# Dilated q and k of the first two batches in rows of eight, masks made by GpSimd, and batch 0's sums in banks of their own

## The chip, the cores and the metric

One core of one Trainium2 chip. The metric is the device time of one execution in microseconds (us). A kernel is timed in several rounds, each beside the kernel before on the same chip; a median is quoted with the lowest and highest run.

## The reference

Eight batches, eight heads, 576 tokens of 64 values. Heads 0 to 3 look back over 32 tokens ("plain"), heads 4 to 7 over every fourth of the last 128 ("dilated"). The output of the attention goes through a feed-forward block with a gate.

```python
mask_plain = (rel >= 0) & (rel < window)                 # rel = query - key, window = 32
mask_dil = (rel >= 0) & (rel < window * dilation) & (rel % dilation == 0)   # dilation = 4
scores = np.where(masks, scale * q @ k.T, -1e9)          # heads 0-3 plain, 4-7 dilated
attn = softmax(scores) @ v
x = attn.transpose(0, 2, 1, 3).reshape(B * S, H * D)     # 4608 x 512
g = x @ w_gate                                           # 512 x 1536
out = (gelu(g) * (x @ w_val)) @ w_out                    # 1536 x 512
```

## The kernel before

The tokens go through the feed-forward in nine chunks of 512. PE (TensorE) works on the attention of the next batch between the matmuls of a chunk. Batch 0's attention has nothing to hide behind, so it is a serial start: load q and k, cast to f16, transpose on PE, add the mask as a bias by a matmul, scores, exp on ScalarE, denominators and numerators on PE, normalisation on DVE (VectorE). The weights come in three pairs (gate and value) and three output blocks, issued by GpSimd's queue. Batch 1's q and k wait for the second pair (`gate`), so that they are not in flight beside it (it lands at 31.2 us, k's load follows at 31.64).

```python
def quads(src, b, h0, lo, hi):                 # four tokens in a partition: 1 KB runs, 128 partitions
    return src[b, h0 : h0 + HK, lo:hi, :].rearrange("h (p r) d -> p h (r d)", r=4)

for t, src, eng in ((0, q, nc.sync), (1, k, nc.scalar)):
    eng.dma_start(out=first_p[:, t], in_=sixes(src, 0))            # plain heads
nc.gpsimd.dma_start(ident, id_dram.ap())                           # constants come by DMA
nc.gpsimd.dma_start(mask_p, mp_dram.ap())
for t, src, eng in ((0, q, nc.sync), (1, k, nc.scalar)):
    eng.dma_start(out=fh(first_d[t]), in_=quads(src, 0, HK, 0, 4 * P))
    eng.dma_start(out=fh(first_r[t]), in_=quads(src, 0, HK, 4 * P, S))   # the last 64 tokens
nc.gpsimd.dma_start(ident32, id32_dram.ap())
nc.gpsimd.dma_start(mask_d, md_dram.ap())
# ... v, tiles
warm(16, 7)
# ... casts and transposes of the plain heads; bias_p by DVE, bias_d by GpSimd
load_v_dil_rest(0)
load_w(0)
v_cast(0, sv0)                                  # waits for v
copy("pool", tiles["v", 0][1], r4(first_vd))
w1 = load_w(1)
load_w(2)
# ...
emit_s(0, 4, pe_mask=True)                      # scores and exp of head pair 0
emit_s(1, 0, pe_mask=True)
# ... casts of dilated k
den(0, 4, wide=True)
# ... t_dil, t_rest: transposes of the dilated heads
den(1, 4, wide=True)
emit_s(2, 0, pe_mask=True)
num(0, 4)
# ...
gate["dma"] = w1
for t, src in ((0, q), (1, k)):
    gated(nc.sync.dma_start(out=st1[:, t], in_=sixes(src, 1)))
qd1, rd1 = load_qk_dil(1)                       # rows of four, cast in the DMA
load_wo(0)
# ... GpSimd casts q and k of batch 1 (needs st1)
wo1 = load_wo(1)
wo2 = load_wo(2)
```

The softmax here doesn't subtract the row's maximum and nothing guards it: scores larger than these inputs give would overflow.

Of the kernel before, what the change touches and what calls it, by code (L numbers as in the profile page):

```python
# [9 lines left out]
F16 = mybir.dt.float16  # L10
F32 = mybir.dt.float32
# [4 lines left out]
WIN = 32  # L16
DIL = 4
USCALE = 32.0


def _np_masks():
    p = np.arange(128)[:, None]

    def band(n, off=0):
        rel = np.arange(n)[None, :] + off - p
        return (rel >= 0) & (rel < WIN)

    main_p, last_p, tail_p = band(160), band(128), band(64, 64)
    main_d = band(128)

    rel = 48 + np.arange(16)[None, :] - p % 64
    rest_d = [(rel >= 0) & (rel < WIN) & (p // 64 == m) for m in range(2)]
    mp = np.concatenate([main_p, main_p, main_p, last_p, tail_p], axis=1).astype(np.float16)
    md = np.concatenate([main_d, rest_d[0], main_d, rest_d[1]], axis=1).astype(np.float16)
    return mp, md
# [3 lines left out]
def kernel(  # L39
# [19 lines left out]
    R6 = S // 6  # L59
    NCH = NT // CH  # L60
# [10 lines left out]

    mp_np, md_np = _np_masks()
    mp_dram = nc.inline_tensor(mp_np, name="mask_plain")
    md_dram = nc.inline_tensor(md_np, name="mask_dil")
    id_dram = nc.inline_tensor(np.eye(P, dtype=np.float16), name="attn_identity")
    id32_dram = nc.inline_tensor(np.eye(16, dtype=np.float32), name="identity_f32")
# [14 lines left out]
    ident32 = const.tile([16, 16], F32, tag="ident32")  # L91
# [20 lines left out]
    first_d = [x32[t][:, 0 : HK * 4 * D] for t in range(2)]  # L112
    first_r = [x32[2 + t][0:16, 0 : HK * 4 * D] for t in range(2)]
# [28 lines left out]
    def fh(t):  # L142
        return t.rearrange("p (h c) -> p h c", h=HK)

    def sixes(src, b):

        return src[b, 0:HK, :, :].rearrange("h (p r) d -> p h (r d)", r=6)

# [126 lines left out]
    def t_dil(b, hp, qd, q0, k0, engs):  # L275

        qtd_ = tiles["qT", b][1]
        for t, c0 in ((0, q0), (1, k0)):
            for hl in range(2):
                for m in range(2):  # L280
                    nc.tensor.transpose(
                        ps16f[:, c0 + (2 * hl + m) * P : c0 + (2 * hl + m + 1) * P],
                        qd[:, t, 2 * hp + hl, 2 * m : 2 * m + 2, :].rearrange("p r d -> p (r d)"),
                        ident,
                    )
        for t, c0 in ((0, q0), (1, k0)):
            copy(
                engs[t],
                qtd_[:, t, 2 * hp : 2 * hp + 2].rearrange("p h m i -> p (h m) i")[:, :, 0:P],
                ps16f[:, c0 : c0 + 512].rearrange("p (c i) -> p c i", i=P),  # L290
            )

    def t_rest(b, hp, rd, r0):

        qtd_ = tiles["qT", b][1]
        f32 = rd[0].dtype == F32
        pv = (psf if f32 else ps16f)[:, r0 : r0 + P]
        for t in range(2):
            for hl in range(2):
                for m in range(2):  # L300
                    c0 = (4 * t + 2 * hl + m) * 16
                    h0 = (2 * hp + hl) * 4 * D + 2 * m * D
                    nc.tensor.transpose(
                        pv[:, c0 : c0 + 16], rd[t][:, h0 : h0 + P], ident32 if f32 else ident[0:16, 0:16]
                    )
        nc.vector.tensor_copy(
            qtd_[:, :, 2 * hp : 2 * hp + 2].rearrange("p t h m i -> p t (h m) i")[:, :, :, P:NCL],
            pv.rearrange("p (t c i) -> p t c i", t=2, i=16),
        )
# [226 lines left out]
    nc.gpsimd.dma_start(ident, id_dram.ap())  # L536
    nc.gpsimd.dma_start(mask_p, mp_dram.ap())
    for t, src, eng in ((0, q, nc.sync), (1, k, nc.scalar)):
        eng.dma_start(out=fh(first_d[t]), in_=quads(src, 0, HK, 0, 4 * P))
        eng.dma_start(out=fh(first_r[t]), in_=quads(src, 0, HK, 4 * P, S))  # L540
    nc.gpsimd.dma_start(ident32, id32_dram.ap())
    nc.gpsimd.dma_start(mask_d, md_dram.ap())
# [5 lines left out]
    qd0 = ldp.tile([P, 2, HK, 4, D], F16, tag="qd", name="qd0")  # L548
    new_qt(0)



    def r4(t):
        return fh(t).rearrange("p h (r d) -> p h r d", r=4)

    warm(16, 7)
    for hp in range(2):
        for t in range(2):
            cast_six(("dve", "act")[t], q6, first_p, t, hp)
    nc.vector.tensor_scalar(bias_p, mask_p, 1.0, 60000.0, ALU.subtract, ALU.mult)  # L560
    for hp in range(2):
        t_plain(0, q6, hp, 2 * hp, ("act", "dve"))
    nc.gpsimd.tensor_scalar(bias_d, mask_d, 1.0, 60000.0, ALU.subtract, ALU.mult)
    for hp in range(2):
        copy("pool", qd0[:, 0, 2 * hp : 2 * hp + 2], r4(first_d[0])[:, 2 * hp : 2 * hp + 2])
    load_v_dil_rest(0)
    load_w(0)
    v_cast(0, sv0)
    copy("pool", tiles["v", 0][1], r4(first_vd))
    w1 = load_w(1)  # L570
    load_w(2)
# [8 lines left out]

    emit_s(0, 4, pe_mask=True)
    emit_s(1, 0, pe_mask=True)
    for hp, eng in ((0, "dve"), (1, "act")):
        copy(eng, qd0[:, 1, 2 * hp : 2 * hp + 2], r4(first_d[1])[:, 2 * hp : 2 * hp + 2])
    den(0, 4, wide=True)
    for hp in range(2):
        t_dil(0, hp, qd0, 4096 + 1024 * hp, 4608 + 1024 * hp, ("act", "dve"))
    for hp in range(2):
        t_rest(0, hp, first_r, P * hp)
    last_keys(0, 0, HK)  # L590
    den(1, 4, wide=True)
    emit_s(2, 0, pe_mask=True)
    num(0, 4)
    den(2, 4, wide=True)
    emit_s(3, 0, pe_mask=True)
    num(1, 4)
    den(3, 4, wide=True)
    num(2, 0)
    num(3, 2)

# [7 lines left out]
    qd1, rd1 = load_qk_dil(1)  # L608
# [28 lines left out]
    for c in range(NCH):  # L637
# [11 lines left out]
        for nb in range(NNB):  # L649
            if nb == 0 and c < 2:  # L650
                ffn1_two(c, (4, 6) if c == 0 else (6, 0))
            elif nb == 0 and late == "x":
                ffn1_two(c, pairs)
            elif nb > 1 or c > 2 and late != "x":
                ffn1(c, nb, pairs[(nb + swap) % 2])
            if pend is not None:
                norm_x(pend, SB)
                pend = None
            if nb in pv_at:
                pend = pv_at[nb]  # L660
                emit_pv(pend, SB, wide=True)
                norm_r(pend, SB, wide=True)
            if c == 0 and nb in (9, 10):
                t_plain(1, q61, nb - 9, 4 + 2 * (nb - 9), ("act", "dve"))
            if c == 0 and nb in (8, 11):
                rr = rd1.rearrange("p t h r d -> p t (h r d)")
                hp = nb // 11
                t_dil(1, hp, qd1, 4096 + 512 * hp, 5120 + 512 * hp, ("dve", "dve"))
                t_rest(1, hp, (rr[:, 0], rr[:, 1]), 6144 + P * hp)
            if nb == NNB - 1 and c > 0 and s_list:  # L670
                n = s_list.pop(0)
                masks.append(emit_s(n, SB, pe_mask=n in biased))
# [106 lines left out]
```

## Time and profile before

| | before |
|---|---|
| time, three runs | 363.44 us (363.22 to 364.12) |
| span in the profile | 362.5 us |
| PE busy | 95% of the span |
| first 16 feed-forward matmuls end | 29.85 us |
| first matmul with the output weights | 51.26 us |
| first feed-forward matmul of the second chunk | 69.03 us |

The last three rows are the milestones. They are read from PE's timeline (start, duration, operation; the wait before it in brackets). Between them lie the serial start, the first chunk's gate and value products, and its output products. In the prediction, the page's busy slices are fortieths of the span; the chain is the work that ended last, followed back to what released it. Of PE's waits up to 70 us, these are three of the four that the profile puts down to a load, as the last releaser, with total, number and longest (the fourth, for batch 1's dilated k, is 0.4 us):

```profile
PE ps L264 <- DMA ident<-attn_identity: 1.4, 1, 1.4
PE ps L281 <- DMA qd<-in_q_dram: 0.9, 1, 0.9
PE ps L512 <- DMA wo<-in_moe_w_out_dram: 0.7, 1, 0.7
```

The first stands in the start, the other two in the first chunk, where batch 1's dilated q and the last output weight are late.

### The profile page before, as it was taken

The numbers are of one execution on the slowest core, as the hardware profiler recorded it, in microseconds if no ns is written. First come the engines' busy times: TensorE is split into PE (matmuls) and PEld (weight loads), VectorE is DVE, ScalarE is ACT, GpSimd is POOL, SyncE is SP. The second block draws the span as 40 slices with busy tenths as digits, with TensorE's granted clock in tenths as the row PEclk, the third lists the DMA queues.
The fourth block names the chain that finished last, engine by engine and source line by source line (L and its number), as shares of the span: only waits on it lengthen the run. The fifth ranks groups of instructions, "written<-read, shape, count | busy, mean of one in ns | idle before, by whom it ended". The sixth has DMA issues, their size and how long they took to land.

```text
span 362.5 us, 6061 instructions
## 1 busy us (share of the span) xinstructions
PE 345.5 (95%) x2400; PEld 164.2 (45%) x2400; DVE 184.8 (51%) x278; ACT 146.0 (40%) x212; POOL 78.2 (22%) x110
## 2 busy tenths in 40 slices
PE   7879899999989999899999999999999999999995
PEld 2554354444544445444444444444444444444442
DVE  1585445744266325864477638783669413303320
ACT  1733255253543345434553356336542223312321
POOL 2580333540432332063003410240000000000000
PEclk9899999999999999999999999999999999999999
DMA  7999999999899898599438962893100030011002
GB/s 184 244 177 214 220 133 194 192 157 235 188 142 204 181 161 154 136 173 135 101 93 186 158 96 89 195 140 72 60 30 2 0 116 2 1 60 58 0 29 89
DMA packets 107292, 45.31 MB, mean 125 GB/s; under 512 B 83040, under 2 KB 102496, under 8 KB 107264
## 3 DMA queue, kind: packets, MB, share of 16 engines
q1 hardware_dynamic: 84272, 31.21, 39.8%
q0 software_dynamic: 21456, 12.01, 26.6%
q10 hardware_dynamic: 1536, 1.70, 2.0%
q8 instruction: 19, 0.31, 0.4%
q14 instruction: 9, 0.07, 0.1%
HBM read 40.13 MB, written 9.44 MB: 137 GB/s over the span
## 4 chain that ended last, share of the span: by engine, by line
PE 78%; DMA 13%; DVE 5%; POOL 2%; ACT 1%; issue 1%; ACTq 0%; SPq 0%; POOLq 0%; DVEq 0%
PE ps L481 41%; PE ps L512 25%; PE ps L433 5%; DMA xT<-in_k_dram 4%; DMA st<-in_k_dram 3%; PE ps L493 3%; DMA wv<-in_moe_w_val_dram 3%; DMA wo<-in_moe_w_out_dram 2%; DVE xT L469 2%; PE ps L360 1%; DMA sv<-in_v_dram 1%; PE ps L330 1%; DVE dt L451 1%; DVE rb L455 1%; PE ps L346 1%; POOL qp L251 1%
## 5 line engine op out<-in xcount | busy, mean ns | idle before, releaser
L506 DVE SCALAR_TENSOR_TENSOR u_all<-g,ps 128x512 f16<-128x512 f16 x108 | 73.5, 686 | 85.9 <-PE ps L481 76.9
L505 ACT ACTIVATE g<-ps 128x512 f16<-128x512 f32 x108 | 63.6, 597 | 126.0 <-PE ps L481 115.0
L512 PE MATMUL ps<-wo,u_all 128*128 128x512 f16 x432 | 101.1, 380 | 1.1 <-DMA wo<-in_moe_w_out_dram 0.7
L481 PE MATMUL ps<-xT,wg 128*128 128x512 f16 x392 | 100.7, 379 | 0.3
L481 PE MATMUL ps<-xT,wv 128*128 128x512 f16 x392 | 100.6, 379 | 0.0
L512 PEld LDWEIGHTS <-u_all 128*128 128x128 f16 x432 | 39.2, 98 | 45.4 <-issue 1.5
L481 PEld LDWEIGHTS <-wv 128*128 128x128 f16 x392 | 38.4, 98 | 46.4 <-issue 0.2
L481 PEld LDWEIGHTS <-wg 128*128 128x128 f16 x392 | 37.2, 98 | 45.0 <-issue 2.1
L523 ACT ACTIVATE osb<-ps 128x512 f32<-128x512 f32 x33 | 19.7, 597 | 49.0 <-PE ps L512 49.0
L451 DVE STREAM_TRANSPOSE dt<-ps 128x576 f32<-128x576 f32 x32 | 24.9, 779 | 26.2 <-PE ps L433 25.9
L190 POOL CAST qp<-st 128x2048 f16<-128x2048 f32 x6 | 11.4, 1894 | 99.0 <-DMA st<-in_k_dram 84.8
L455 DVE STREAM_TRANSPOSE rb<-rc 128x576 f32<-128x576 f32 x32 | 24.9, 778 | 1.1
L362 ACT ACTIVATE P<-ps 128x1152 f16<-128x1152 f32 x16 | 18.1, 1130 | 10.8 <-PE ps L360 10.8
L340 ACT ACTIVATE P<-ps 128x960 f16<-128x960 f32 x16 | 15.5, 970 | 10.7 <-PE ps L330 10.6
L469 DVE TENSOR_TENSOR xT<-ps,rb 128x576 f16<-128x576 f32 x16 | 17.9, 1126 | 0.3
L493 PE MATMUL ps<-xT,wg 128*128 128x512 f16 x40 | 15.2, 379 | 2.1 <-DVE xT L469 1.6
L525 DVE TENSOR_SCALAR osb<-ps 128x512 f32<-128x512 f32 x3 | 2.1, 691 | 28.8 <-PE ps L512 28.8
L433 PE MATMUL ps<-P,ones 128*64 128x96 f16 (+5 forms) x216 | 14.3, 245 | 1.6 <-ACT P L362 1.6
L493 PE MATMUL ps<-xT,wv 128*128 128x512 f16 x40 | 15.2, 379 | 0.0
L466 DVE TENSOR_TENSOR xT<-ps,rb 128x576 f16<-128x576 f32 x16 | 11.8, 745 | 0.3
L370 DVE TENSOR_TENSOR P<-P,mask_p 128x1344 f16<-128x1344 f16 x10 | 8.4, 852 | 6.8 <-ACT P L341 6.8
L370 DVE TENSOR_TENSOR P<-P,mask_d 128x1152 f16<-128x1152 f16 x8 | 6.1, 757 | 11.1 <-ACT P L362 11.1
(75 smaller groups left out, 244.2 us busy)
## 6 DMA issues: line engine op xcount, KB each, us to landing
out_dram<-osb SPq DMA_DIRECT2D x36, 256.0 KB, 2.1
sv<-in_v_dram SPq DMA_DIRECT2D x40, 128.0 KB, 3.2
st<-in_q_dram SPq DMA_DIRECT2D x24, 128.0 KB, 3.7
st<-in_k_dram SPq DMA_DIRECT2D x24, 128.0 KB, 3.1
qd<-in_q_dram POOLq DMA_DIRECT2D x7, 256.0 KB, 5.0
qd<-in_k_dram POOLq DMA_DIRECT2D x7, 256.0 KB, 6.9
vd<-in_v_dram POOLq DMA_DIRECT2D x7, 256.0 KB, 7.2
wg<-in_moe_w_gate_dram POOLq DMA_DIRECT2D x3, 512.0 KB, 7.4
```

The source lines that it names most:

```text
L340: nc.scalar.activation(pt[:, :, 0:PB], sb[:, 0, :, 0:PB], AF.Exp, bias=0.0, scale=scale)
L362: nc.scalar.activation(pt, ps[:, b0 : b0 + 4, 0:DW], AF.Exp, bias=0.0, scale=scale)
L433: nc.tensor.matmul(o, lhs, rhs, start=st, stop=True, skip_group_check=True)
L451: nc.vector.transpose(dst, den)
L455: nc.vector.transpose(rb.rearrange("p (b c) -> p b c", c=32), bass.AP(tensor=rc.tensor, offset=rc.offset, ap=[rc.ap[0], [1, 18], [0, 32]]),)
L469: nc.vector.tensor_tensor(dst.rearrange("p (i m s) -> p i m s", m=2, s=2), num, rb.rearrange("p (s m i) -> p i m s", s=2, m=2), ALU.mult,)
L481: nc.tensor.matmul(ps[:, b0 + gi, :], w[:, kc, ns], xT[kc][:, tok], start=(kc == 0), stop=(kc == NKC - 1))
L493: nc.tensor.matmul(ps[:, pairs[nb] + gi, :], w[:, kc, ns], xT[kc][:, tok], start=(kc == 0), stop=(kc == NKC - 1),)
L505: nc.scalar.activation(g, ps[:, b0, :], AF.Gelu)
L506: nc.vector.scalar_tensor_tensor(u_all[:, nb, :], g, USCALE, ps[:, b0 + 1, :], ALU.mult, ALU.mult)
L512: nc.tensor.matmul(ps[:, bank, :], u_all[:, fc, tb * P : (tb + 1) * P], wo_t[fc // 4][:, fc % 4, :], start=(fc == 0), stop=(fc == NNB - 1),)
L523: nc.scalar.activation(osb, ps[:, bank, :], AF.Copy, bias=0.0, scale=1.0 / USCALE)
```

## The change

Four parts with one intent, an earlier start: fewer and longer runs for dilated q and k; no constants over the DMA engines; more warm-up; sums that don't wait for one another's PSUM banks. The order of the weight loads moves with them.

```diff
-    nc.gpsimd.dma_start(ident, id_dram.ap())          # and mask_p, ident32, mask_d
+    nc.gpsimd.memset(ident, 1.0)
+    for sign in (1, -1):
+        nc.gpsimd.affine_select(out=ident, in_=ident, pattern=[[sign, P]], ...)
+    band(mask_p[...], 0, 0) ...                        # ten more selects
+    nc.gpsimd.tensor_scalar(bias_p, mask_p, 1.0, 60000.0, ALU.subtract, ALU.mult)   # was on DVE
 [...]
-        eng.dma_start(out=fh(first_d[t]), in_=quads(src, 0, HK, 0, 4 * P))
-        eng.dma_start(out=fh(first_r[t]), in_=quads(src, 0, HK, 4 * P, S))
+    for g in range(2):                                 # rows of eight: 72 partitions, 2 KB runs
+        for t, src, eng in ((0, q, nc.sync), (1, k, nc.scalar)):
+            eng.dma_start(out=first_d[t][g]..., in_=eights(src, 0, HK + 2 * g, HK + 2 * g + 2))
 [...]
-    warm(16, 7)
+    warm(20, 7)
 [...]
+    cast_d("pool", 0, 0)
+    cast_d("dve", 1, 0)
+    cast_d("act", 1, 1)          # ScalarE: second half of k, ahead of the exps
+    cast_d("dve", 0, 1)
     load_v_dil_rest(0)
     load_w(0)
-    v_cast(0, sv0)
-    copy("pool", tiles["v", 0][1], r4(first_vd))
     w1 = load_w(1)               # no longer behind v's casts
-    load_w(2)
 [...]
+    def num_split(n, b0):        # ScalarE copies out of PSUM, GpSimd multiplies
+        emit_pv(n, b0, ("num",))
+        nc.scalar.copy(first_n[n], psf[:, b0 * 512 : b0 * 512 + S])
+        nc.gpsimd.tensor_tensor(xT[n][:, 0:S], first_n[n], rb, ALU.mult)
     emit_s(0, 4, pe_mask=True)
     emit_s(1, 0, pe_mask=True)
+    t_dil(0, 0, qd0, 4, ("dve", "dve"))     # transposes of 72 columns, no remainders
+    t_dil(0, 1, qd0, 6, ("act", "act"))
 [...]                                       # v's casts
+    den(0, 0, wide=True)
+    den(1, -2, wide=True)
+    emit_s(2, 4, pe_mask=True)
+    emit_s(3, 0, pe_mask=True)
+    den(2, 4, wide=True)
+    num_split(0, 4)
+    num_split(1, 4)
     den(3, 4, wide=True)
     num(2, 0)
     num(3, 2)
+    load_w(2)                    # third pair behind GpSimd's products
 [...]
-    qd1, rd1 = load_qk_dil(1)
+    nc.gpsimd.dma_start(out=qd1[:, t]..., in_=eights(src, 1, HK, H))   # q and k of batch 1
```

## The prediction

> **What bounds the kernel now.** I read the page first: PE is busy for 95% of 362.5 us, so only time in which PE lacks work can be won. The chain's summary says the same and names the exceptions.
>
> ```profile
> PE   7879899999989999899999999999999999999995
> DMA  7999999999899898599438962893100030011002
> PE 78%; DMA 13%; DVE 5%; POOL 2%; ACT 1%; issue 1%; ACTq 0%; SPq 0%; POOLq 0%; DVEq 0%
> ```
>
> PE's thin slices lie at the start, and there the DMA engines are full; the DMA part of the chain (13%) lies there too. So I read the chain in order of time up to 54 us, where it turns into PE for good.
>
> ```profile
> 1.19 12.94 DMA xT<-in_k_dram
> ...
> 14.15 4.48 DMA sv<-in_v_dram
> ...
> 18.84 1.04 POOL vp L177
> ...
> 21.95 9.26 DMA wv<-in_moe_w_val_dram
> ...
> 31.64 11.45 DMA st<-in_k_dram
> ...
> 43.15 2.37 POOL qp L251 x3
> ...
> 46.20 8.15 DMA wo<-in_moe_w_out_dram
> ```
>
> What to see: one load releases the next. Dilated k lands at 14.1, only then does the queue issue the last v load; v lands at 18.6; GpSimd casts v, and only then issues the second weight pair (21.2, 21.95); its landing at 31.2 releases batch 1's q and k (landed 43.1); their casts hold up the last output weight, which lands at 54.35. PE waits for that last one by 0.7 us. All of this ends 54 us into the run; after it PE is dense apart from waits that the change does not touch.
>
> Next the timeline of the first 30 us, for the work itself.
>
> ```profile
> 9.27 0.41 PE L264 MATMUL ps<-ident,qp 96*128 96x96 f16 x6 [1.36 <-DMA ident<-attn_identity]
> 11.13 1.32 PE L323 MATMUL ps<-bias_p,ident 128*128 128x480 f16 x4
> 14.15 0.66 DVE L253 CAST qd<-xT 128x512 f16<-128x512 f32 x1 [2.03 <-DMA xT<-in_k_dram]
> 19.39 0.65 PE L346 MATMUL ps<-bias_d,ident 128*128 128x288 f16 x4
> 25.19 0.39 PE L493 MATMUL ps<-xT,wg 128*128 128x512 f16 x1
> 27.79 0.38 PE L493 MATMUL ps<-xT,wg 128*128 128x512 f16 x1 [0.67 <-DVE xT L469]
> ```
>
> PE waits 1.36 us for an identity that comes by DMA; dilated q and k are usable at 14; the first dilated scores start at 19.4; the feed-forward starts at 25.2, but its first 16 matmuls need DVE's last product and end at about 29.6. Last, stretches of 1 us:
>
> ```profile
> 10.00:11.00 1.00, 0.95 (x17) 0.81 (x18) 0.69 (x2) 1.00 (x2) 0.02 (x1) 0.81 1.08 342
> 11.00:12.00 1.00, 1.00 (x8) 0.58 (x6) 0.94 (x2) 0.69 (x2) 1.00 (x1) 0.50 1.18 249
> 45.00:46.00 1.00, 1.00 (x7) 0.44 (x5) 0.00 (x0) 0.60 (x1) 1.00 (x2) 1.00 0.10 15
> ```
>
> The granted clock (third from the end) is 0.50 from 10.8 to 14.0: four bias matmuls take 1.32 us. And at 45 us the DMA engines, saturated before, stand nearly idle (share 0.10): the last weights are not yet issued, because GpSimd is casting.
>
> [...]warm-up matmuls start 0.43 us apart, the spacing shortens near 7.1, the clock is halved from 10.8 to 14.0, that is for 3.2 us.
> [...]18 to 19 us, with v's 256-byte rows, moves 137 GB/s at a share of 1.63; 10 to 11 moves 342 at 1.08.
>
> **The change part by part.**
> *Masks and identity.* Gone are 273 KB of early loads (32+168+72+1): at the 250 GB/s of those stretches about 1 us of DMA, so plain q and k land near 7.6 and 8.4 instead of 8.3 and 9.05. In its place GpSimd works. Copies there cost about 0.27 us plus 0.75 ns per column (0.43 at 256, 1.04 at 1024); bias_d cost 1.19 us at 288 columns, so about 3.2 ns per column. With 1 ns per column for a select (my guess between these): identity 0.8, plain mask 3.0, bias_p 0.27 + 672 x 3.2 ns = 2.4, dilated mask 1.8, bias_d 1.2, and the cast of half of q 1.04: together 10.2 us. From 1.3 us on,[...] bias_p is ready at 7.5 and the cast near 12[...].
> *Rows of eight.* 2 KB runs instead of 1 KB for 2.3 MB (two batches), the 16-row remainders and their 16 transposes gone. 16 transposes of 72 columns per head pair against 8 of 128 plus 8 of 16: PE even within 0.2 us. First-batch halves land at about 10.2 and 11.8 instead of 14: 2.3 us earlier on the chain's first link; v's last loads are issued earlier too.
> *Warm-up 16 to 20.* PE then works until about 8.75, just before the first casts end: the clock may stay full, saving about half of the two bias groups, 1.2 us, if bias_p is there.
> *Own banks.* Both plain denominators go to banks of their own, scores 2 and 3 use both halves, two of the four final products leave DVE (2 x 0.72 us) for ScalarE copies (0.65 each) and GpSimd products (about 1.5 each, an estimate from two inputs at twice a copy).
> *Weights.* The second pair is issued directly behind the first, no longer behind v's casts; the third goes behind the GpSimd products.
>
> [...]scores 0 at 11.4, exp 0 and 1 done at 15, dilated copies by 16.3, scores 2 at 16.3. DVE then sets the end: key copy 0.4, four normalisations of 1.85 (0.78+0.27+0.78) = 7.4, two products 2.1, from 15.5 on: 25.4 to 26.1, and the first 16 matmuls end at about 27.0, 2.6 us earlier than 29.6. The weight pair is issued near 16.5 instead of 21.95 and lands near 27 instead of 31.2; batch 1's q, k then about 40; the last weight near 51.3 instead of 54.35. PE reaches that weight at 54.4 - 2.6 - 1.3 (its waits at 42 to 43) = 50.5, waits a little, and both views give 3 us: 360.4.
>
> [...]
>
> I put 0.6 on the faster case (the warm-up was lengthened by only four matmuls, and bias_p moved to GpSimd, which makes sense only if GpSimd is early), and get 0.6 x 360.4 + 0.4 x 362.8 = 361.4.
>
> **The rivals.**
> *GpSimd becomes the bound at the start*[...]. For: ten selects, two slow bias computations and a cast in one queue, and every score of batch 0 needs bias_p. Against: 7.4 us of that engine were idle. Time: 362.8, with slow selects (2 ns per column, 2 us more) 364 to 365.
> *The start is faster but the loads decide anyway.* For: the chain is DMA up to 54 us and the share is over 1 throughout. If the third weight pair, now behind GpSimd's products, arrives late for the ninth column block (needed near 38), the gain is given back there: 362 to 363. Against: the hole at 45 us shows that the DMA engines have slack that earlier issues can use.
> *Everything falls into place*, including the full clock and no wait for the last weight: 4 to 5 us, 358.5 to 359.5.
>
> **Range and chances.** 80%: 358.8 to 364.2. Nothing after 55 us changes except by being moved, so a gain of 7.3 us (2%) needs more than the whole sum above: 3%. A loss as large needs a start of over 10 us more on GpSimd: 2%. Within 2%: 95%.
>
> **What would show it.** The start of the plain bias matmuls: near 10.8 (no wait on GpSimd) in the faster case[...]. Dilated casts released at 10 to 12. The last of the first 16 feed-forward matmuls near 27, DVE ending the wait in front of them. The landing of the second weight pair near 27, the last output weight near 51. A clock of 1.0 from 10 to 14. I am wrong if the start moves little and the time still falls, or if the first matmuls come earlier and a later wait in the first chunk grows by as much.

The sum is 0.6 x 360.4 + 0.4 x 362.8 = 361.4. 362.8 was worked out from a wait of GpSimd ahead of its first work, an assumption that no trace here shows. That the longer warm-up keeps the clock full (1.2 us of the faster case) is not shown: with 16 matmuls the clock was at 0.50 from 10.6 to 14.0 us in the kernel before, and at 1.00 from 9 to 14 in the run with the banks alone.

## The result and the profile after

| | runs | median, us | lowest to highest |
|---|---|---|---|
| before | 4 | 363.78 | 363.22 to 364.22 |
| after | 4 | 364.33 | 363.90 to 364.54 |

The ratio is 1.0014 with a 95% interval of 0.9995 to 1.0034: the same time. A ratio is the mean time of one kernel's fast runs over that of the other's fast runs of the same rounds, so it is not quite the ratio of the medians. The time lies just above the predicted range, and 2.9 us above the predicted value.

The page of the kernel after, with the parts that answer to those of before:

```profile
PE   7589999999989999899999999999999999999995
DMA  8998999999999991599539952893100030011002
PE 87%; DMA 5%; DVE 5%; ACT 2%; issue 1%; ACTq 0%; SPq 0%; DVEq 0%
```

The second slice of PE, 9 to 18 us, is thinner than before (5 against 8). The chain is now PE from much earlier on: DMA's share fell from 13% to 5%. So a chain of loads was shortened, and still nothing was won. GpSimd's timeline and PE's, in the start:

```profile
1.09 0.65 POOL L95 TENSOR_SCALAR_AFFINE_SELECT ident<-ident 128x128 f16<-128x128 f16 x2
4.88 2.48 POOL L116 TENSOR_SCALAR bias_p<-mask_p 128x672 f16<-128x672 f16 x1
11.30 1.03 POOL L264 CAST qd<-xT 72x1024 f16<-72x1024 f32 x1 [0.35 <-DMA xT<-in_q_dram]
...
10.45 0.73 PE L318 MATMUL ps<-bias_p,ident 128*128 128x480 f16 x4
16.63 1.98 PE L295 MATMUL ps<-ident,qd 72*128 72x72 f16 x32 [3.97 <-ACT P L335]
```

GpSimd is early: its first select starts at 1.09 us, bias_p is done at 7.36, and the plain bias matmuls start at 10.45 at the full clock. Then PE waits 3.97 us for the exp of the first scores. ScalarE's timeline says why:

```profile
14.66 1.04 ACT L262 CAST qd<-xT 72x1024 f16<-72x1024 f32 x1 [3.47 <-DMA xT<-in_k_dram]
15.62 0.96 ACT L335 ACTIVATE P<-ps 128x960 f16<-128x960 f32 x1
```

The first exp needs only scores that were ready soon after 11 us, but it stands in ScalarE's queue behind the cast of k's second half, and that half lands at 14.64 us. The DMA engines bring the halves slowly. The stretch from 9 to 11 us (columns: stretch, its length, busy time of PE, its weight loads, DVE, ACT and POOL with counts, granted clock, DMA share, GB/s; the DMA share sets the time of all packets against that of 16 engines, so it can exceed 1), first of before, then of after:

```profile
9.00:11.00 2.00, 1.43 (x23) 1.16 (x24) 1.03 (x3) 1.95 (x3) 0.02 (x1) 0.91 1.08 344
```

```profile
9.00:11.00 2.00, 1.50 (x22) 1.09 (x22) 1.09 (x2) 2.00 (x4) 1.79 (x4) 1.00 1.10 229
17.00:30.00 13.00, 11.77 (x129) 7.89 (x127) 10.00 (x17) 7.16 (x9) 6.93 (x8) 0.50 1.06 175
29.00:30.00 1.00, 1.00 (x4) 0.31 (x3) 1.00 (x2) 0.00 (x0) 1.00 (x2) 0.50 0.02 6
```

229 GB/s against 344, with the engines just as full. The second line shows the clock behind PE's idle stretch: it is 0.50 for the rest of the start (16.8 to 30.5 us). That this stretch alone brings the clock down is not shown: without such a wait the clock is also at 0.50 from 15.9 to 29.6 us in the run with all but the rows of eight, and from 16.0 to 29.7 us in a second trace of the kernel before (below). The third is a hole in the loads, because the third weight pair is now issued behind GpSimd's products. The feed-forward's first and sixteenth matmul:

```profile
27.88 0.61 PE L488 MATMUL ps<-xT,wg 128*128 128x512 f16 x1
32.40 0.38 PE L488 MATMUL ps<-xT,wv 128*128 128x512 f16 x1
```

The milestones, each column worked out from the starts and durations in the timelines:

| | before | after | after minus before |
|---|---|---|---|
| first 16 feed-forward matmuls end | 29.85 | 32.78 | +2.93 |
| from there to the first output matmul | 21.41 (to 51.26) | 19.17 (to 51.95) | -2.24 |
| from there to the second chunk | 17.77 (to 69.03) | 17.41 (to 69.36) | -0.36 |
| sum | | | +0.33 |

In these two traces the start lost what the first chunk gained. How the loss and the gain are shared out depends on the trace, though. The run with loads alone, further below, is the kernel before up to its end, so it left a second trace of it. There the sixteenth matmul and the first of the second chunk are:

```profile
31.41 0.38 PE L493 MATMUL ps<-xT,wv 128*128 128x512 f16 x1
68.98 0.39 PE L493 MATMUL ps<-xT,wg 128*128 128x512 f16 x1
```

The same start ends 1.94 us later, at 31.79, with the clock at 0.50 for longer, and yet the second chunk begins at the same place. Against this trace the changed kernel loses 0.99 us in the start and regains 0.61.

In the first chunk PE's two waits for batch 1's dilated q and k (0.91 and 0.36 us) are gone. With them goes PE work: the transposes of a pair of batch 1's dilated heads took 1.02 and 0.83 us, with the remainders of 16 rows, and take 0.52 each in rows of eight. So 1.27 of the 2.24 us are waits for loads and about 0.8 are shorter transposes. Later, among the output products, the wait for the last output weight is gone as well. Up to 54 us after 32.78, the only PE wait left is one of 0.26 us for DVE.

### The profile page after: what moved, and what is told of

It reads as the page before. It is cut to its first block, busy times and chain, and to the rows that moved or that the text cites. A ratio compares the mean times of both kernels' runs of the same rounds, so it can differ in the third digit from the quotient of the medians.

```text
span 362.8 us, 6082 instructions
## 1 busy us (share of the span) xinstructions
PE 347.0 (96%) x2404; PEld 165.6 (46%) x2404; DVE 185.4 (51%) x272; ACT 147.6 (41%) x214; POOL 85.6 (24%) x122
## 3 DMA queue, kind: packets, MB, share of 16 engines
q0 software_dynamic: 20896, 11.74, 25.9%
## 4 chain that ended last, share of the span: by engine, by line
PE 87%; DMA 5%; DVE 5%; ACT 2%; issue 1%; ACTq 0%; SPq 0%; DVEq 0%
PE ps L476 46%; PE ps L507 25%; PE ps L428 6%; PE ps L488 4%; DMA xT<-in_k_dram 3%; DMA out_dram<-osb 2%; PE ps L355 1%; PE ps L325 1%; DVE xT L464 1%; PE ps L341 1%; DVE dt L446 1%; DVE rb L450 1%; PE ps L295 1%; PE ps L318 1%; DVE u_all L501 1%
## 5 line engine op out<-in xcount | busy, mean ns | idle before, releaser
L464 DVE TENSOR_TENSOR xT<-ps,rb 128x576 f16<-128x576 f32 x16 | 17.9, 1126 | 0.4
L488 PE MATMUL ps<-xT,wv 128*128 128x512 f16 x40 | 15.9, 398 | 0.0
L428 PE MATMUL ps<-P,ones 128*64 128x96 f16 (+5 forms) x216 | 15.2, 258 | 0.0
L190 POOL CAST vp<-sv 128x1024 f16<-128x1024 f32 x8 | 8.7, 1090 | 11.9 <-DMA sv<-in_v_dram 11.9
## 6 DMA issues: line engine op xcount, KB each, us to landing
wo<-in_moe_w_out_dram POOLq DMA_DIRECT2D x3, 512.0 KB, 10.2
```

The costliest lines, as they stand in the source:

```text
L428: nc.tensor.matmul(o, lhs, rhs, start=st, stop=True, skip_group_check=True)
L464: nc.vector.tensor_tensor(dst.rearrange("p (i m s) -> p i m s", m=2, s=2), num, rb.rearrange("p (s m i) -> p i m s", s=2, m=2), ALU.mult,)
L488: nc.tensor.matmul(ps[:, pairs[nb] + gi, :], w[:, kc, ns], xT[kc][:, tok], start=(kc == 0), stop=(kc == NKC - 1),)
```

## The experiments

Two accounts stood against each other at first. **Q**, the queue: the late exp (and the clock at 0.50 that is seen behind it) costs the start 3 us; put right, the whole time falls. **L**, the loads: the last loads of the first chunk set the time, so that a start of any speed ends in the same place. A third question came with the traces: why rows of eight arrive so slowly.

### The exps ahead of ScalarE's cast

```diff
-    cast_d("act", 1, 1)
 [...]
     emit_s(1, 0, pe_mask=True)
+    cast_d("act", 1, 1)
```

> The changed kernel with one line moved: ScalarE casts the second half of dilated k behind the two exponentials of the plain heads instead of in front of them. Theory Q (a cast that waits for a late load blocks ScalarE's queue): the first exponential starts near 11.7 us instead of 15.6, PE's wait of 4.0 us in front of the dilated transposes falls to under 2 us, the granted clock stays above 0.9 on average over 0 to 28 us, the last of the first 16 feed-forward matmuls ends near 29 us instead of 32.6, and the time falls by 2.5 to 4 us to about 361. Rival L (the late load itself bounds the start, whoever casts it): the end of these 16 matmuls moves by less than 1 us and the time by less than 0.5.

Measured: 365.70 us (362.98 to 368.07), ratio 1.0042 (1.0007 to 1.0077). The start is what Q said: the first exp at 11.68 us, the first feed-forward matmul at 24.38, the sixteenth done at 28.86, 3.9 us earlier than in the changed kernel. The time is not. The chain of this run:

```profile
16.35 14.10 DMA wv<-in_moe_w_val_dram
...
30.88 11.97 DMA st<-in_k_dram
42.91 2.37 POOL qp L264 x3
...
45.98 8.46 DMA wo<-in_moe_w_out_dram
```

The third weight pair is issued 3 us sooner than in the changed kernel (25.6) and competes with the second pair, which lands at 30.45 instead of 28.98. Batch 1's k waits for that, GpSimd's casts for k, the last output weight for the casts; it lands at 54.43. PE waits 2.8 us for output weights, 0.8 for batch 1's dilated k, and 0.7 for the second pair. Behind the wait for the last weight the clock is at 0.50 from 53.5 to 60.3 us; from the first output matmul to the second chunk PE takes 22.8 us instead of 17.4, of which the waits are 2.8 and most of the rest is that clock. So the start's gain is given back as waits for loads, and more is lost with the clock behind them. That speaks for L. (The profiled run was among the slow ones of a wide spread.)

### The gap filled with warm-up matmuls

```diff
     emit_s(0, 4, pe_mask=True)
+    warm(16, 3)
     emit_s(1, 0, pe_mask=True)
```

> The changed kernel with 16 matmuls on ones put between the scores of the first and of the second plain pair; ScalarE's queue as in the change, so the first exponential still starts near 15.6 us. Theory C (half of the loss is the clock, [...]): the clock stays at 1.0 after 16 us, the 16 first feed-forward matmuls end at about 30.5 instead of 32.6, and the time falls by about 1.5 to 2 us to 362.5. Rival (the clock costs nothing since DVE's chain sets the end of this stretch): no movement of that end, time unchanged within 0.5 us.

Measured: 364.18 us (363.29 to 364.88), ratio 0.9998 (0.9984 to 1.0013). The clock is 1.00 throughout and the sixteenth matmul is done at 30.27, 2.5 us earlier than in the changed kernel, with the exps as late as there. So the halved clock, not the idle time alone, made most of the late start in that trace. Yet batch 1's k lands at 42.37, the last output weight at 53.91, PE waits 0.9 and 0.6 us for them, and the time stays. A second start that is earlier and buys nothing.

### The masks alone

The kernel before with the identities, masks and biases made by GpSimd, nothing else:

```diff
-    nc.gpsimd.dma_start(ident, id_dram.ap())     # and mask_p, ident32, mask_d
+    # memsets, selects, bias_p and bias_d on GpSimd, as in the change
```

> The kernel before with only the masks and identities made by GpSimd (both biases there too), nothing else changed. Prediction on record: plain q and k land 0.7 us earlier and dilated q and k about 1 us earlier than 13.9 and 14.1, PE's wait of 1.36 us for the identity goes, the feed-forward starts about 1 us earlier: 362.5. Rival (the loads behind the masks fill the freed time with v's short rows and the chain through v stays): dilated loads land at 13.5 or later, time within 0.5 us of before.

Measured: 363.03 us (361.88 to 365.71), ratio 0.9976 (0.9947 to 1.0005): a small gain at most, not shown at this interval. PE's wait in front of its first transposes stays at 1.4 us, now put down to q's cast instead of the identity. Dilated q and k land at 13.2 and 13.59 instead of 13.9 and 14.13; the waits for dilated k (0.6) and for the output weight (0.4) are a little shorter.

### The rows of eight alone

```diff
-        eng.dma_start(out=fh(first_d[t]), in_=quads(src, 0, HK, 0, 4 * P))   # and first_r
+            eng.dma_start(out=first_d[t][g]..., in_=eights(src, 0, HK + 2 * g, HK + 2 * g + 2))
 # t_dil and batch 1's loads as in the change; masks, banks, weights as before
```

> The kernel before with only dilated q and k of batches 0 and 1 read in rows of eight tokens (72 partitions, 2 KB runs, halves of two heads), masks still loaded, order of work as before. Prediction on record: first halves land near 11, second halves near 13 (with the masks' loads still there), 1 to 2 us less in the end. Rival S ([...]the longer runs gain nothing): halves land at 12 and 15 or later, GB/s between 7 and 12 us near 230 as in the change and not near 280 as before, time unchanged or 0.5 to 1 us longer.

Measured: 367.87 us (366.06 to 370.44), ratio 1.0104 (1.0075 to 1.0133), slower by 1%. The second halves land at 16.1 to 16.3, behind the constants; v follows at 21.1, the second weight pair at 33.0, batch 1's dilated k at 45.85, for which PE waits 1.6 us. The part of the change that was to shorten the chain's first link lengthens every link.

### Rows of twelve

Theory K of the expectation was that loads of 72 partitions have fewer of the DMA engines at work than loads of 48. What the traces show is 12 packets of 4 bytes for each load of 72 partitions and 16 for each of 48 (in the loads alone, below). If that is what costs the rate, rows of twelve (48 partitions, 3 KB runs) should run faster. Its rival P is that the rate follows the number of partitions.

```diff
-    def eights(src, b, h0, h1):  ... r=8
+    def eights(src, b, h0, h1, n=8):  ... r=n        # n=12 for batch 0
```

> The changed kernel with dilated q and k of batch 0 read in rows of twelve tokens (48 partitions, 3 KB runs, same bytes) instead of eight (72 partitions, 2 KB). Theory K ([...]): between 9 and 11 us the rate is near 340 GB/s instead of 240, the second half of k lands near 12.5 to 13 instead of 14.6, the first exponential starts 1 us earlier than 15.6 although the cast is longer (1.5 instead of 1.04 us). Rival P ([...]longer runs do not help): rate at or under 240, landing at 14.6 or later. The time of the whole kernel should move by less than 1 us in either case, as the loads behind it decide.

Measured: 366.35 us (366.05 to 366.55), ratio 1.0067 (1.0043 to 1.0092).

```profile
9.00:11.00 2.00, 1.18 (x23) 0.91 (x20) 0.96 (x2) 1.99 (x3) 1.78 (x3) 1.00 1.06 146
```

146 GB/s, slower still; k's second half lands at 16.50, the first exp starts at 17.96, PE waits 5.9 us for it. So K, by which it should have risen, is not the main cause. The time moved by 2 us, not by less than 1 as expected: the sixteenth matmul is done at 34.79 and the second chunk begins at 71.36, both 2.0 us later than in the changed kernel, so a start that is later still is carried through in full. Longer runs on fewer partitions go with lower rates: 344, 229, 146.

### Rows of eight in two loads of four tokens

Rows of eight differ from rows of four in both partitions and length of run. This run keeps 72 partitions and goes back to 1 KB runs.

```diff
-            eng.dma_start(out=first_d[t][g]..., in_=eights(...))
+            for x in range(2):
+                eng.dma_start(out=...[:, x], in_=eights(...)[:, :, x * 4 * D : (x + 1) * 4 * D])
```

> The changed kernel, but each of the four loads of rows of eight is made as two loads of four tokens each: 72 partitions as in the changed kernel, but runs of 1 KB as in the kernel before. Theory P (the rate follows the number of partitions): 9 to 11 us carries 210 to 240 GB/s as in the changed kernel, the second half of k lands at 14 to 15.5, exp 0 starts at 15 to 16.5, time 364 to 365. Rival R (the long run itself costs the rate): 310 GB/s or more, the second half of k lands before 13.5, exp 0 starts before 14.5 and the first 16 feed-forward matmuls end a microsecond or more before 32.6.

Measured: 363.99 us (363.68 to 364.33), ratio 1.0003 (0.9987 to 1.0019).

```profile
9.00:11.00 2.00, 0.00 (x0) 0.00 (x0) 0.00 (x0) 0.58 (x1) 1.78 (x4) 1.00 0.85 201
```

201 GB/s: runs of 1 KB don't bring the 344 back, so the long run is not what costs the rate (R falls; P's band for the rate was missed low, at a DMA share of 0.85). The second effect was not intended: with two more loads to issue, ScalarE's queue comes to its first cast only at 11.71 us instead of 8.56, so the times of the exps say nothing about the rate. What the run shows beside it is again L: the sixteenth matmul is done at 30.45, 2.3 us earlier than in the changed kernel, and the second chunk begins at 69.12 against 69.36.

### The lower and the upper half of the partitions

Rows of four reach 128 partitions, rows of eight 72, rows of twelve 48, and both q and k start at partition 0. The rates of 344, 229 and 146 GB/s can follow the number of partitions (P) or the place where they lie (D). The test: q stays in 0 to 47 and k goes to 64 to 111. Rows of eight cannot be moved in this way, since 72 rows don't fit into 64 partitions; rows of twelve can.

```diff
-    first_d = [[x32[2 * t + g][0:R12, 0 : 24 * D] ...
+    first_d = [[x32[2 * t + g][64 * t : 64 * t + R12, 0 : 24 * D] ...
 # the f16 tile and the transposes' identity for k from partition 64 as well
```

> The changed kernel with rows of twelve for batch 0's dilated q and k, as the run with rows of twelve, but k goes to partitions 64 to 111 and q to 0 to 47. Theory D ([...]): 9 to 11 us carries 230 to 320 GB/s instead of 146, the second half of k lands before 14.5 us instead of 16.5, exp 0 starts before 15.5 instead of 17.96, the time is 363.5 to 365. Rival P (each load's number of partitions sets its rate, wherever they lie): about 146 GB/s again, landing at 16 to 17, 366 to 366.7 us.

Measured: 363.17 us (363.09 to 363.65), ratio 0.9973 (0.9955 to 0.9991).

```profile
9.00:11.00 2.00, 1.39 (x21) 1.09 (x22) 1.04 (x3) 2.00 (x4) 1.84 (x4) 1.00 1.03 254
```

254 GB/s instead of 146, with the same number of loads, runs and partitions; nothing but the place of k differs. k's second half is usable at 13.24 us instead of 16.5, the first exp starts at 14.73 instead of 17.96. The rate is inside the expected 230 to 320. By the packets' records a run of 3 KB takes 0.20 us in the median of this stretch instead of 0.35. In this kernel the rate of these loads depends on which partitions they reach (146 with both in 0 to 47, 254 with k in 64 to 111); P falls. The time is below the expected 363.5 to 365, and its interval lies under 1: with the exps still late, the sixteenth matmul is done at 31.58, 1.2 us earlier than in the changed kernel, PE waits for no load in the first chunk, and the second chunk begins at 68.46, 0.9 us earlier.

### Loads alone

Behind the end of the kernel before, rounds of nothing but loads of dilated q and k, each waiting for the last.

```diff
+    for n, p0 in ((4, 0), (8, 0), (8, 56), (12, 0), (12, 64), (6, 0), (6, 32)) * 2:
+        last = probe(n, p0, last)       # q into partitions from 0, k from p0, rows of n tokens
```

> The kernel before, and behind its end 14 rounds of nothing but loads: each round brings dilated q and k of one batch (four loads, 1.0 to 1.2 MB) and waits for all. Rows of four over 128 partitions; of eight over 72, both from partition 0; of eight, k from 56; of twelve over 48, both from 0; of twelve, k from 64; of six over 96, both from 0; of six, k from 32; all twice. Theory D[...]: k moved up makes the rounds of eight and of twelve shorter by a quarter or more (from about 5 to 3.5 us of transfer and from 7 to 4), near the rows of four; rows of six lie between. Rival P (the number of partitions alone): moving k changes no round by more than 5%. The result stays correct; its time says nothing.

The second seven rounds but the rows of six, from first to last packet: rows of four; of eight from 0, then k from 56; of twelve from 0, then k from 64 (columns as in the stretches above). The result of the kernel was correct; the time (462.45 us) holds the rounds.

```profile
409.58:413.10 3.52, 0.00 (x0) 0.00 (x0) 0.00 (x0) 0.00 (x0) 0.00 (x0) 0.50 0.94 297
414.57:420.62 6.05, 0.00 (x0) 0.00 (x0) 0.00 (x0) 0.00 (x0) 0.00 (x0) 0.50 0.72 195
422.18:427.96 5.78, 0.00 (x0) 0.00 (x0) 0.00 (x0) 0.00 (x0) 0.00 (x0) 0.50 0.73 204
429.76:437.29 7.53, 0.00 (x0) 0.00 (x0) 0.00 (x0) 0.00 (x0) 0.00 (x0) 0.50 0.96 156
439.17:445.92 6.75, 0.00 (x0) 0.00 (x0) 0.00 (x0) 0.00 (x0) 0.00 (x0) 0.50 0.87 174
```

This is a miss of D in size. k moved up makes the rounds of eight shorter by 4% (6% in the first seven) and those of twelve by 10% (14%), not by a quarter. Rows of six went from 247 to 249 GB/s. Two things can be read. For 72 partitions the share of 0.72 is 11.5 of 16 engines busy; for 48 from partition 0 it is 0.96, that is 15.4. The packets' records have 48 packets of 4 bytes in a round of rows of eight, 12 for each of its four loads, and 64 in every other round, 16 for each. That fits 12 engines at work for 72 partitions, and the place of k doesn't change it (0.72 and 0.73). For 48 partitions a packet falls from 0.32 to 0.23 us in the median, as inside the kernel, but the share falls too (0.96 to 0.87). So two things went with the low rate of rows of eight, the place of the partitions (4 to 6% here) and the lower share; how much each costs them inside the kernel is not shown, as k was moved there in rows of twelve alone. Why rows of twelve gain 74% in rate inside the kernel (146 to 254) and 12 to 16% alone (156 to 174, 154 to 179) was not tested. The landings point to the order: inside the kernel the first halves of q and k land 0.2 us apart (10.77 and 10.98), in the last round shown 1.1 us apart (442.62 and 443.69), so q's and k's loads ran less side by side there.

### The banks and the new order alone

```diff
 # before, with: num_split, scores 2 and 3 in both halves of PSUM, all
 # transposes ahead of the denominators, load_w(2) behind the products
```

> The kernel before with only the new order of the sums of batch 0 (both plain denominators in banks of their own, scores 2 and 3 in the two halves, final products of heads 0 to 3 split over ScalarE and GpSimd, third weight pair issued behind those products). Prediction on record: DVE loses 1.4 us of products and the feed-forward's first 16 matmuls end up to 1 us earlier than 29.6. Rival W (the late third weight pair and the GpSimd products only shift the loads): that end moves by under 0.5 us, the second weight pair lands about 2 us earlier because the third is not beside it, time within 0.5 us of before.

Measured: 364.80 us (363.27 to 365.80), ratio 1.0022 (0.9996 to 1.0048). The first exp starts at 11.64 instead of 13.16, but that is the clock, at 1.00 where it was 0.50 before (10.6 to 14.0); the edit touches nothing ahead of it. Batch 1's dilated k is issued at 28.41 instead of 24.88 and lands at 43.9; PE waits 1.2 and 1.1 us for batch 1's dilated q and k instead of 0.9 and 0.4. What the new order gives at the start cannot be told from this trace.

### All but the rows of eight

```diff
 # before, with the masks by GpSimd, the banks and order of the change, warm(20, 7)
```

> The changed kernel with rows of eight undone in both batches (rows of four and the remainder of 16 rows as before); masks by GpSimd, warm-up of 20 and the banks stay. If the rows of eight are what costs the change its gain (theory K and the longer wait in ScalarE's queue), dilated loads land near 13.4 and the time is 362 or less, 2 us under the changed kernel. Rival (the loads of batch 1 decide whatever happens at the start): within 0.7 us of the kernel with the masks alone (363.0).

Measured: 364.05 us (363.04 to 364.93), ratio 1.0004 (0.9981 to 1.0028). The first exp starts at 11.74, dilated q and k land at 12.7 and 12.98, and the last output weight lands at 54.95, later than before; PE waits 0.8 us for it. This is no early start, though: with the clock at 0.50 from 15.9 to 29.6 us the sixteenth matmul is done at 32.03, 0.75 us before that of the changed kernel. So undoing the rows of eight brings the exps forward by 3.9 us and doesn't bring the predicted gain.

### The output weights ahead of GpSimd's casts

If the loads at the end of the first chunk take the start's gain, then it should come back when the last two output weights no longer stand behind GpSimd's casts for batch 1, which wait for k. The edit, with the early exps:

```diff
     load_wo(0)
+    wo1 = load_wo(1)
+    wo2 = load_wo(2)
     q61 = ...                        # GpSimd's casts of batch 1
-    wo1 = load_wo(1)
-    wo2 = load_wo(2)
```

> The kernel of e1 (exponentials first) and, in addition, the second and third output weights issued in front of GpSimd's casts of batch 1 instead of behind them. Theory D (since e1 the time hangs on the chain second weight pair, q and k of batch 1, GpSimd casts, output weights, landing at 54.4): the last output weight lands by 50, PE's waits of 2.8 us for it go, the clock does not drop at 55 us, the time falls by 3 to 4.5 us from e1's 365.7 to about 361.5. Rival B (the DMA engines are full anyway, order does not matter): the output weights land earlier but q and k of batch 1 later than 43, PE waits for those instead, time within 1 us of e1.

Measured: 363.11 us (362.45 to 364.18), ratio 0.9981 (0.9955 to 1.0007); with the exps early alone it was 365.70. The second chunk begins at 68.03 instead of 69.36, and PE no longer waits for output weights. What is left:

```profile
PE ps L295 <- DMA qd<-in_k_dram: 1.3, 1, 1.3
```

```profile
28.86 14.71 DMA qd<-in_k_dram
```

Batch 1's dilated k, issued at 28.86 behind the third pair, is the last load to hold PE up: the first line is from PE's waits, the second from the chain.

The control is the same edit on the changed kernel, with the exps late:

```diff
 # after, cast_d("act", 1, 1) ahead of the exps as given
+    wo1 = load_wo(1)                 # and wo2, ahead of the casts of batch 1
```

> The changed kernel with nothing but the two last output weights issued ahead of GpSimd's casts for batch 1; the exps stay late. Theory C (in the changed kernel PE has no wait from 32.6 to 52 us, so the output weights decide nothing there, and the early start and the early weights pay only together): ratio 0.998 to 1.002 against the kernel before, the last output weight lands 2 us or more before it does in the changed kernel and PE's end of the first chunk stays at 51 to 52.5 us. Rival (the order of the weights alone gives what the run with both gave): 363.1 or less, ratio 0.998 or below.

Measured: 364.37 us (363.13 to 366.84), ratio 1.0021 (0.9994 to 1.0047), just above the band of 0.998 to 1.002. The loads' order alone gives nothing, because PE has no wait for them there. The four corners:

| median, us | output weights late | output weights early |
|---|---|---|
| exps late | 364.33 (after) | 364.37 |
| exps early | 365.70 | 363.11 |

By the medians neither step gains alone, and together they are worth 1.2 us; by the ratios the two ends of that, 1.0014 (0.9995 to 1.0034) and 0.9981 (0.9955 to 1.0007), still touch. The corner with the exps alone holds the clock at 0.50 behind the wait for a weight. The milestones say more than the times:

| | sixteenth matmul done | second chunk begins | between |
|---|---|---|---|
| before | 29.85 | 69.03 | 39.18 |
| before, second trace | 31.79 | 68.98 | 37.19 |
| change as given | 32.78 | 69.36 | 36.58 |
| rows of twelve | 34.79 | 71.36 | 36.57 |
| output weights early | 32.57 | 69.15 | 36.58 |
| twelves in both halves | 31.58 | 68.46 | 36.88 |
| gap filled | 30.27 | 68.89 | 38.62 |
| exps early | 28.86 | 71.92 | 43.06 |
| exps and output weights early | 30.01 | 68.03 | 38.02 |

Where the start is late, what follows takes 36.6 us and the start sets the time (Q). Where it is much earlier, what follows takes longer, as PE waits for loads (L). The changed kernel is on the first side, and close to the second: of the 1.2 us that the halves of twelve win at the start 0.9 are left at the second chunk, of the 2.5 us of the filled gap 0.5.

### Versions that beat both kernels

The kernel before with the masks by GpSimd and the output weights early, then the same with the longer warm-up:

```diff
 # before, with the masks by GpSimd, wo1 and wo2 ahead of the casts
-    warm(16, 7)
+    warm(20, 7)                      # second of the two
```

> The kernel before with masks, identities and biases made by GpSimd, and the two last output weights issued ahead of the casts for batch 1. Theory: the masks' part gains about 0.7 us (363.03 was measured), and the waits for the output weights that stayed there (0.4 us) go: 362.2 to 363.0, ratio 0.995 to 0.998, with a wait of about 0.6 to 1.5 us for batch 1's dilated k as what remains. Rival (the weights issued sooner delay batch 1's q and k by as much): 363.0 to 364, waits for dilated or plain q and k of 1.5 us or more.

Measured: 362.27 us (361.10 to 363.54), ratio 0.9955 (0.9933 to 0.9978), as expected. PE waits 0.2 us for dilated k, less than expected.

> As the run with the masks by GpSimd and the output weights early, with the warm-up lengthened from 16 to 20 matmuls, as the change has it. Theory: the clock stays at 1.0 from 10.8 to 14 us (0.5 with 16 matmuls), so the four bias matmuls take 0.7 us instead of 1.3 and the start gains at most 1 us; but the time is set by the loads of the first chunk, so the total moves by less than 0.4 us against that run: 362 to 363. Rival (the start counts where the output weights are early): 0.8 us or more below that run, 361.5 to 362.

Measured: 361.94 us (361.10 to 363.02), ratio 0.9946 (0.9927 to 0.9966). Against the run with 16 the difference of 0.33 us is within the scatter. The four bias matmuls took 0.73 us at the full clock in both, so the comparison with a halved clock that the theory named did not arise.

The repaired change, with rows of twelve in both halves, the exps early and the output weights early:

```diff
 # after, with rows of twelve, k from partition 64
 # cast_d("act", 1, 1) behind emit_s(1, ...); wo1 and wo2 ahead of the casts
```

> The changed kernel with rows of twelve in both halves of the partitions, the exps of scores 0 and 1 ahead of ScalarE's cast, and the last output weights ahead of the casts of batch 1. Against the run with the exps and the weights early and rows of eight (363.11 us): theory D says that the loads up to 15 us are done a microsecond earlier, so v and the second weight pair are too: 362.0 to 363.0, ratio against the kernel before 0.994 to 0.9975. Rival (the gain is lost again behind batch 1's dilated k, for which PE waited 1.3 us there): 363 to 363.6.

Measured: 361.55 us (361.39 to 362.67), ratio 0.9931 (0.9913 to 0.9949), below the expected 362.0 to 363.0. ScalarE's first exp, the last load in the chain, and the start of the second chunk:

```profile
11.34 0.97 ACT L341 ACTIVATE P<-ps 128x960 f16<-128x960 f32 x1 [0.42 <-PE ps L331]
```

```profile
28.41 13.71 DMA qd<-in_k_dram
```

```profile
66.50 0.39 PE L494 MATMUL ps<-xT,wg 128*128 128x512 f16 x1
```

The start of the second chunk is 2.5 us earlier than before, the end of the sixteenth matmul (29.50) 0.35 us. PE waits 0.3 us for dilated k instead of 1.3. The intervals of this version and of the one with masks, weights and warm-up overlap, so which of the two is better is not shown; both beat before and after. From the sixteenth matmul to the second chunk this version takes 37.0 us.

| run | median, us | ratio to before |
|---|---|---|
| change as given | 364.33 | 1.0014 |
| exps early | 365.70 | 1.0042 |
| gap filled | 364.18 | 0.9998 |
| masks only | 363.03 | 0.9976 |
| rows of eight only | 367.87 | 1.0104 |
| rows of twelve | 366.35 | 1.0067 |
| banks only | 364.80 | 1.0022 |
| exps and output weights early | 363.11 | 0.9981 |
| all but rows of eight | 364.05 | 1.0004 |
| eights in two loads | 363.99 | 1.0003 |
| output weights early | 364.37 | 1.0021 |
| masks, output weights early | 362.27 | 0.9955 |
| the same, longer warm-up | 361.94 | 0.9946 |
| twelves in both halves | 363.17 | 0.9973 |
| the same, exps and output weights early | 361.55 | 0.9931 |

## Why the prediction was right or wrong

**That the time stays within 2% was right, the value and the range were not:** 361.4 us was predicted, 364.33 came.

**"Masks and identity": right in most terms.** bias_p was put at 7.5 us and is done at 7.36; the cast of q "near 12" ends at 12.33; bias_p's 2.4 us measured 2.48, bias_d's 1.2 measured 1.18. The six selects of the plain mask, put at 3.0, took 2.38, the two of the identity, put at 0.8, took 0.65. The faster case, given 0.6, is the true one. ScalarE's copy was put at 0.65 and GpSimd's product at 1.5; they took 0.64 and 1.40. The slower case rested on a wait ahead of GpSimd's first work; it did not show: the first select starts at 1.09 us, 0.08 us after the end of the memset before it. One reading was wrong: PE's wait of 1.36 us was not for the identity but mostly for q's cast, as shown above. Warm-up: the clock is full from 10 us to 14 as predicted, and the bias matmuls take 0.73 us instead of 1.32. But this is not shown to be the four matmuls more: with 16, they took 0.73 us as well in the second trace of the kernel before and in the run with masks and output weights early. That the step came true may be luck.

**"Rows of eight": this step failed.** "First-batch halves land at about 10.2 and 11.8 instead of 14: 2.3 us earlier." k's second half lands at 14.64. The longer run was taken as a gain, at the DMA rate of before; measured, the rate fell from 344 to 229 GB/s. What the runs showed is the partitions: rows of twelve at 146 GB/s in the lower half and 254 in both, and in the loads alone a share of 0.72 for 72 partitions against 0.96 for 48. Alone, the eights cost 1% (367.87). The transposes, put at even within 0.2 us, became shorter by 0.3 to 0.5 us for each pair of batch 1's heads.

**"Exp 0 and 1 done at 15; scores 2 at 16.3": failed with it.** The order on ScalarE was not followed through: with a cast that waits for the last half ahead of the exps, a late half becomes a PE wait of 3.97 us, and the clock is at half from 17 to 30. Neither step is the whole cause: with the rows of eight undone the first exp is early and the time stays at 364.05. With the layout of the loads, the order on ScalarE and the output weights all put right, 361.55 was measured, near the 361.4 predicted. "The first 16 matmuls end at about 27.0" became 32.78. With the exps in front it is 28.86 in one trace, with the clock at 0.50 until 19.3 us, and 30.01 in another (output weights early as well), with it at 0.50 until 25.6: the term for the queue, its share of the clock included, is 2.8 to 3.9 us, and the remaining 1.9 to 3.0 us over the prediction lie in loads and clock.

**"The weight pair lands near 27, batch 1's q, k about 40, the last weight near 51.3": the landings right within 2 us.** Measured 28.98, 39.34 and 52.6, and PE has no wait for the last weight. The chain of loads was indeed shortened, by 2.2 us for the second pair and 3.8 for batch 1's k, and 1.27 of the 2.24 us that the changed kernel regains in the first chunk are waits for loads that are gone. But this comes from the late start as well: with the exps early, the third pair competes, and k lands at 42.86.

**The rivals.** "The start is faster but the loads decide anyway" described the wrong side for the change as given, where the start is slower and the loads are not what is waited for. It described the repaired starts: the early exps, the filled gap, the eights in two loads. Its sign, a third pair behind the products that comes late, showed in the hole from 28 to 30.5 us. The prediction's last sentence, that it would be wrong if a later wait in the first chunk grew by as much as the first matmuls came earlier, is what the run with the early exps did.

**The chances.** 0.95 within 2% was fair. The range of 358.8 to 364.2 was too narrow above: its rivals included a slow GpSimd, but no slower loads.

## What to carry to other kernels

Before loads are made longer and fewer, look at the rate that the trace shows for each layout, and at which partitions the loads in flight reach together: spreading q and k over both halves gave 254 GB/s where the lower half gave 146. A cast that waits for the last load belongs behind the work that is already fed: with k's cast ahead of it ScalarE's first exp started at 15.62 us, with the cast behind it at 11.68. A faster start pays up to the point where the loads of the next stage end later than the work: here the faster loads alone were worth 0.3% (0.9973), the exps ahead of the cast gained nothing alone, and 1.2 us by the medians with the output weights moved as well. And one trace of a start is not enough: the same start ended at 29.85 and at 31.79 us, by the clock that each trace had.
